# Attention and two feed-forward layers on one core: the first loads, the window bias and the mask of the opening rearranged

## The chip, the cores and the metric

The kernel runs on one core of a Trainium2 chip. The metric is device time in microseconds. Before the change three runs gave a median of 640.09 us (639.93 to 641.4).

The engines are called PE (TensorE, matrix products, with PEld for its weight loads), DVE (VectorE), ACT (ScalarE), POOL (GpSimd) and SP (SyncE, which here only issues DMAs). Each has its own instruction queue and works through it in the order in which the program was written. SPq and ACTq are the queues from which DMAs are issued.

## The reference

Attention over 2 batches, 8 heads, 768 positions and 64 values a head, with a window and a few global keys, then two feed-forward layers over 1536 tokens:

```python
scores = q @ k.T / 8
rel = pos[:, None] - pos[None, :]
is_global = pos[None, :] < n_global          # 8
is_local = (rel >= 0) & (rel < n_local)      # 96
dist = where(is_global & ~is_local, n_local, abs(rel))
slopes = 2.0 ** (-8 * (arange(8) + 1) / 8)
scores = where(is_global | is_local, scores - slopes[h] * dist, -1e9)
x = softmax(scores) @ v                      # then (1536, 512)
h = x @ w_in;   y = max(0.01 * h, h) @ w_out                 # layer 1
h = y @ w2_in;  out = (P(h) / (Q(h) + 1e-6)) @ w2_out        # layer 2, P and Q with coefficients a, b
```

n_global and n_local are 64-bit integers that the kernel reads from memory. The weights come as 64-bit floats and are decoded to 32-bit on the chip.

## The kernel before

A head pair (two heads of one batch) is one of 8 steps of the attention. In a pair, each of 6 blocks of 128 query rows and each of the 2 heads is a unit, 12 units a pair and 96 in all. A unit compares its 128 queries with 128 window columns (block 0) or 256 (32 global keys and the previous block's last 96 in the first half, its own block in the second).

Values are kept in two 32-bit halves, "high" and "low" (qh, ql, kh, kl), so a score is three products: qh·kh, qh·kl, ql·kh (L379). To get there, q and k rows are loaded (L286), transposed on PE with the identity matrix (L308), copied to the high half on ACT (L318, L347), and subtracted for the low half on DVE (L320, L349). `prep_slots` (L336 on POOL, L333 on ACT) then copies the previous block's and the global keys' columns into the free places between the blocks.

A unit's steps are: scores on PE, `least` on DVE (L390, adds the head's bias and takes the least), `exp` on ACT (L404), transposes on PE (L415), `evacuate` on ACT or DVE (L421, L423), `values` on PE (L434 to L437), and `finish` on DVE after every three blocks (L443 to L446). The main loop (L570 to L592) runs over slots n; in slot n it emits scores of n, least of n, exp of n - 1, transposes of n - 3, values of n - 5, and then `fillers(n)`: the loads and preparation of the next pair, one of the six late biases, the decoding of weights. So the order of work on each engine is written out by hand. The two units of a slot share a score bank with the units two slots later, and a group of scores waits for the least before it.

The opening, in program order:

- ACT issues two DMAs that spread the integers over 128 partitions (L92, L93); SP issues eight loads of 96 KB, the first pair's q and k in halves of three blocks, in the order q, q, k, k, q, q, k, k (L458 to L460).
- PE runs 18 products of a constant tile that nothing reads (`keep_busy`, BUSY), later 3, 2 and 2 more at other places.
- the first halves are transposed; then `window_bias` (L213) makes the distances for all 384 columns, reads the integers (L99 to L103), makes a mask of -8e9 beside them and clips the distances. A head's bias is dist times slope plus mask, one DVE instruction over 384 columns (L241). Head 0 comes before the first least, head 1 between the first and the second, heads 2 to 7 in slots 1, 2, 4, 5, 8 and 9.
- after the first halves SP goes on to the second pair's k (2 loads of 192 KB), the first pair's v (6 loads), the second pair's q (2 loads of 192 KB; its buffer is single, so it waits until the first pair's q has been transposed).
- in slot 0 the second halves are transposed; in slot 1 they are copied and subtracted; units 4 and 5 (third block) still work on the first half.
- the second pair's k and q are transposed in slots 4 and 5 (PREP0).

After the attention come the two layers, 96 units of 512 tokens by 128 columns, two product groups a unit (L621, L742, L744).

```python
            for n in range(8):
                next(halves[n // 2 % 2])
            keep_busy(BUSY[0])
            q0, k0, q1, k1 = P_[0].prep_q(0), P_[0].prep_k(0), P_[0].prep_q(1), P_[0].prep_k(1)
```

Of the kernel before, what the change touches and what calls it, by code (L numbers as in the profile page):

```python
# [8 lines left out]
F32 = mybir.dt.float32  # L9
F32R = mybir.dt.float32r  # L10
# [9 lines left out]
MAX_LOCAL = P - GW + 1  # L20
QK_BOUND = 7000.0
EPS_Q = 1.0 + 1e-6


@with_exitstack
def attention_moe_moe2(
# [67 lines left out]
    intf = cpool.tile([P, 4], F32, name="intf")  # L94
    nums = cpool.tile([P, 2], F32, name="nums")
    n_loc = nums[:, 0:1]
    n_glo = nums[:, 1:2]

    def read_ints():  # L99
        nc.vector.tensor_copy(intf, ints)  # L100
        lo, hi = (intf.rearrange("p (j w) -> p j w", w=2)[:, :, w] for w in range(2))
        nc.vector.scalar_tensor_tensor(hi, lo, 0.0, hi, ALU.is_lt, ALU.add)
        nc.vector.scalar_tensor_tensor(nums, hi, 4294967296.0, lo, ALU.mult, ALU.add)  # L103

    coef = cpool.tile([P, 8], F32, name="coef")

# [73 lines left out]
    def decode_all(rpool, dpool, wt, w_in, w_out, f):  # L180
        for m, src in enumerate(weight_srcs(w_in, w_out, f)):
# [6 lines left out]
            split_hi(wt[:, 2 * m, :], t.t)  # L188
            split_lo(wt[:, 2 * m + 1, :], t.t, wt[:, 2 * m, :])

    zeros = cpool.tile([P, 1], F32, name="zeros")
    nc.vector.memset(zeros, 0.0)
    eight = cpool.tile([P, 1], I32, name="eight")
# [18 lines left out]

    def window_bias(bpool, rpool):  # L213


        misc = rpool.tile([P, 2 * DM], I32, tag="raw", name="misc")
        misc2 = rpool.tile([P, 2 * DM], F32, tag="raw", name="misc2")
        rel_i = misc[:, 0:BW]
        dist = misc.bitcast(F32)[:, BW : 2 * BW]
        mask = misc2[:, 0:BW]  # L220
        nc.gpsimd.iota(rel_i[:, 0:W2], [[-1, W2]], base=P, channel_multiplier=1)
        nc.gpsimd.iota(rel_i[:, W2:BW], [[-1, P]], base=0, channel_multiplier=1)
# [8 lines left out]
        read_ints()  # L231

        nc.vector.tensor_scalar(mask, dist, n_loc, -8e9, ALU.is_ge, ALU.mult)
        mask_g = misc2[:, 0 : 2 * W2].rearrange("p (a c) -> p a c", a=2)[:, :, 0:GW]
        col_g = col.unsqueeze(1).to_broadcast([P, 2, GW])
        nc.vector.scalar_tensor_tensor(mask_g, col_g, n_glo, mask_g, ALU.is_ge, ALU.mult)
        nc.vector.tensor_scalar(dist, dist, n_loc, None, ALU.min)
        bias = bpool.tile([P, H, BW], F32, name="bias")

        def head(h):  # L240
            nc.vector.scalar_tensor_tensor(  # L241
                bias[:, h, :], dist, -8.0 * 2.0 ** (-8.0 * (h + 1) / H), mask, ALU.mult, ALU.add
            )

        return bias, head

    def attention(wpool, w1, ffn):
        with ExitStack() as actx:
# [26 lines left out]
            class Pair:  # L275
# [62 lines left out]
                def prep_q(self, s):  # L338
                    if s == 0:
                        self.qt = apool.tile([P, S], F32, tag="qt", name="qt", bufs=1)  # L340
                        self.qh, self.ql = (apool.tile([P, S], F32R, tag=n, name=n) for n in ("qh", "ql"))
                    cs = slice(s * HALF, (s + 1) * HALF)
                    t = self.transposed(self.qr, s).rearrange("p i c -> p (i c)")
                    yield
                    hi, lo, w = self.qh[:, cs], self.ql[:, cs], self.qt[:, cs]
                    if self.n == 0:
                        nc.scalar.activation(hi, t, AF.Copy)  # L347
                        yield
                        nc.vector.tensor_tensor(lo, t, hi.bitcast(F32), ALU.subtract)  # L349
                        return  # L350
# [3 lines left out]
                    nc.gpsimd.tensor_tensor(lo, w, hi.bitcast(F32), ALU.subtract)  # L354

                def x_out(self, s):
                    yield from x_steps(ffn.bank(), self.xp, self.b, self.hp, s)
# [97 lines left out]
                p.st, p.o = {}, {}  # L455
            U = [Unit(n) for n in range(PU * len(pairs))]

            halves = [P_[0].load("qr", q, HB), P_[0].load("kr", k, HB)]  # L458
            for n in range(8):
                next(halves[n // 2 % 2])  # L460
# [10 lines left out]
            q0, k0, q1, k1 = P_[0].prep_q(0), P_[0].prep_k(0), P_[0].prep_q(1), P_[0].prep_k(1)  # L471
            next(q0)
            next(k0)
            next(q0)
            next(k0)
            keep_busy(BUSY[1])
            bias, bias_head = window_bias(bpool, rpool)
            next(q0, None)
            next(k0)
            bias_head(0)  # L480
            next(k0, None)
            P_[1].load_k()
            P_[0].load_v()
            P_[1].load_q()
# [33 lines left out]
            def fillers(n):  # L518
# [21 lines left out]
                if p == 0 and s in BIAS:  # L540
                    bias_head(2 + BIAS.index(s))
# [28 lines left out]
            while n < len(U) or running or n <= len(U) + LV + 1:  # L570

                for m in GROUPS.get(n, ()):
                    for step, _ in enumerate(zip(unit(m).scores(), unit(m + 1).scores())):
# [501 lines left out]
```

## Time and profile before

| | before |
|---|---|
| median of 3 runs | 640.09 us |
| profiled execution, its own time | 639.84 us |
| its span | 638.0 us |
| PE busy | 626.7 us (98%) |
| DVE busy | 472.8 us (74%) |
| ACT busy | 438.1 us (69%) |
| POOL busy | 208.3 us (33%) |

The span is the part of the execution that the profile covers; 1.84 us lie around it. In a timeline row the columns are start, duration, engine, line, operation, output<-inputs, shapes and count, and in brackets the idle time of the engine just before, with what ended it. Times are in us from the start of the span. In a table of stretches the columns are the stretch, its length, each engine's busy time with its count of instructions, the granted PE clock, the mean share of the 16 DMA engines and GB/s (a share can pass 1 where packets overlap).

### The profile page before, as it was taken

Reading aid. Unit: us, or ns where it says so; the run is one execution under the profiler, and the core shown is the slowest. Engines: PE = TensorE matmul, PEld = TensorE weight load, DVE = VectorE, ACT = ScalarE, POOL = GpSimd, SP = SyncE. Lnnn points to the kernel's source line nnn. Section 1 sums busy time; section 2 is a strip of 40 time slices with the busy share of each in tenths; the row PEclk is TensorE's granted clock in tenths of the full one; section 3 lists DMA queues with packets and bytes.
Section 4 is the critical chain, followed back from the end, with each engine's and each line's share of the span. In section 5 each row is a group of like instructions: output and inputs, shape, how many; then the busy total and the mean of one; then the engine's idle time right before and its main releaser. Section 6 shows DMA issues by size and latency. Waiting matters only on the chain.

```text
span 638.0 us, 9653 instructions
## 1 busy us (share of the span) xinstructions
PE 626.7 (98%) x3289; PEld 527.5 (83%) x3289; DVE 472.8 (74%) x934; ACT 438.1 (69%) x829; POOL 208.3 (33%) x221
## 2 busy tenths in 40 slices
PE   7999999999999999999999999999999999999996
PEld 6999998888888888888888888888888888888884
DVE  6888897887886555555444479897777777897784
ACT  5888987877866545455333477876677888876672
POOL 3978874344543434332000012222222222112220
PEclk9999999999999999999999999999999999999999
DMA  9876751755167776765222300000023331100001
GB/s 192 190 174 154 184 137 67 271 180 207 58 205 249 217 229 200 235 210 181 92 96 95 100 33 34 1 1 1 0 97 102 98 95 48 67 25 1 2 1 72
DMA packets 81179, 73.35 MB, mean 115 GB/s; under 512 B 51232, under 2 KB 67616, under 8 KB 81120
## 3 DMA queue, kind: packets, MB, share of 16 engines
q1 hardware_dynamic: 80320, 71.19, 37.6%
q0 software_dynamic: 224, 0.92, 0.4%
q8 instruction: 28, 0.46, 0.3%
q10 hardware_dynamic: 576, 0.53, 0.2%
q14 instruction: 31, 0.25, 0.1%
HBM read 60.69 MB, written 11.93 MB: 114 GB/s over the span
## 4 chain that ended last, share of the span: by engine, by line
PE 94%; DVE 3%; SPq 1%; DMA 1%; issue 0%; ACT 0%; DVEq 0%; ACTq 0%
PE h L621 41%; PE y L744 21%; PE y L742 20%; PE pt L415 3%; PE sc L379 3%; PE o L437 2%; PE o L436 2%; PE h L308 1%; SPq L286 1%; DVE sn L390 1%; PE h L204 1%; DMA qr<-in_q_dram 1%; DVE xl L210 0%; DVE pts L423 0%; PE o L434 0%
## 5 line engine op out<-in xcount | busy, mean ns | idle before, releaser
L621 PE MATMUL h<-xh,w 128*128 128x512 f32 x768 | 252.8, 390 | 0.0
L621 PEld LDWEIGHTS h<-xh,w 128*128 128x128 f32 x768 | 144.2, 188 | 29.7
L621 PE MATMUL h<-xl,w 128*128 128x512 f32 x384 | 149.4, 389 | 0.0
L675 POOL TENSOR_TENSOR gl<-u,gh 128x512 fp32r<-128x512 f32 x44 | 57.0, 1296 | 264.6 <-PE y L744 125.6
L742 PE MATMUL y<-gh,w 128*128 128x512 f32 x384 | 126.0, 389 | 0.0
L744 PE MATMUL y<-w,gh 128*128 128x512 f32 x384 | 125.5, 389 | 0.0
L160 POOL TENSOR_TENSOR dec<-dec,wraw 128x512 int32<-128x512 int32 x48 | 63.8, 1339 | 82.8 <-DVE wraw L147 79.1
L621 PEld LDWEIGHTS h<-xl,w 128*128 128x128 f32 x384 | 72.1, 188 | 14.8
L742 PEld LDWEIGHTS y<-gh,w 128*128 128x128 f32 x384 | 72.0, 188 | 14.9
L744 PEld LDWEIGHTS y<-w,gh 128*128 128x128 f32 x384 | 72.1, 188 | 14.8
L744 PE MATMUL y<-w,gl 128*128 128x512 f32 x192 | 75.1, 391 | 0.0
L742 PE MATMUL y<-gl,w 128*128 128x512 f32 x192 | 74.7, 389 | 0.0
L646 DVE TENSOR_TENSOR gl<-h,gh 128x512 fp32r<-128x512 f32 x48 | 33.0, 688 | 52.5 <-ACT gh L645 52.5
L645 ACT ACTIVATE gh<-h 128x512 fp32r<-128x512 f32 x48 | 28.6, 597 | 59.8 <-PE y L742 56.5
L697 ACT ACTIVATE h<-h 128x512 f32<-128x512 f32 x48 | 28.7, 597 | 52.6 <-PE h L621 52.5
L641 DVE SCALAR_TENSOR_TENSOR h<-h,g 128x512 f32<-128x512 f32 x48 | 33.3, 694 | 27.2 <-ACT g L640 27.0
L685 DVE SCALAR_TENSOR_TENSOR w<-w,epsq,h 128x512 f32<-128x512 f32 (+1 forms) x49 | 36.4, 743 | 20.9 <-ACT h L709 20.3
L640 ACT ACTIVATE g<-h 128x512 f32<-128x512 f32 x48 | 28.8, 600 | 31.1 <-PE h L621 30.9
L404 ACT ACTIVATE pr<-sn,st 128x256 f32<-128x256 f32 (+1 forms) x96 | 47.5, 496 | 1.3 <-DVE st L390 1.1
L699 DVE SCALAR_TENSOR_TENSOR w<-h,coef,w 128x512 f32<-128x512 f32 x48 | 35.9, 748 | 15.9 <-ACT w L698 15.6
L744 PEld LDWEIGHTS y<-w,gl 128*128 128x128 f32 x192 | 36.0, 188 | 8.7 <-POOL gl L675 1.1
L742 PEld LDWEIGHTS y<-gl,w 128*128 128x128 f32 x192 | 36.1, 188 | 7.5
(115 smaller groups left out, 1123.9 us busy)
## 6 DMA issues: line engine op xcount, KB each, us to landing
wraw<-in_moe_w_in_dram SPq DMA_DIRECT2D x24, 512.0 KB, 4.7
wraw<-in_moe_w_out_dram SPq DMA_DIRECT2D x24, 512.0 KB, 4.6
scratch<-dec SPq DMA_DIRECT2D x32, 256.0 KB, 5.3
wf<-scratch SPq DMA_DIRECT2D x16, 512.0 KB, 3.4
w<-in_moe_w_in_dram SPq DMA_DIRECT2D x8, 512.0 KB, 4.2
w<-in_moe_w_out_dram SPq DMA_DIRECT2D x8, 512.0 KB, 5.0
vc<-in_v_dram SPq DMA_DIRECT2D x16, 192.0 KB, 3.2
qkraw<-in_q_dram SPq DMA_DIRECT2D x6, 512.0 KB, 3.5
```

What stands on the lines that cost most here:

```text
L160: nc.gpsimd.tensor_tensor(ti, ti, self.c, ALU.add)
L404: nc.scalar.activation(self.pr[:, :w], self.sn[:, :w], AF.Exp, bias=self.least_at, scale=-1.0,)
L621: nc.tensor.matmul(h, wt[:, m, c * P : (c + 1) * P], xs[:, c, cs], start=c == 0 and n == 0, stop=c == NK - 1 and n == 2,)
L640: nc.scalar.activation(g, h, AF.Copy)
L641: nc.vector.scalar_tensor_tensor(h, h, 0.01, g, ALU.mult, ALU.max)
L646: nc.vector.tensor_tensor(gl, h, gh.bitcast(F32), ALU.subtract)
L675: (nc.gpsimd if on_pool else nc.vector).tensor_tensor(gl, g, gh.bitcast(F32), ALU.subtract)
L685: nc.vector.scalar_tensor_tensor(ow[:, cs], ow[:, cs], epsq, oh2[:, cs], ALU.add, ALU.mult)
L697: nc.scalar.activation(h2, h, AF.Square)
L699: nc.vector.scalar_tensor_tensor(w0, h2, coef[:, 7:8], w0, ALU.mult, ALU.add)
L742: nc.tensor.matmul(ys[d], wt[:, m, ds_], gs, start=st, stop=sp)
L744: nc.tensor.matmul(ys[d], gs[:, ds_], wt[:, m, :], start=st, stop=sp)
```

## The change

- The integers come to one partition only (two loads of one row), are put together there, and a product of a row of ones with them on PE spreads them over 128 partitions (`spread`, copied to `nums` by DVE).
- The first pair's q and k come in parts of two and four blocks instead of three and three, in the order q, k, k, q; of the first k part one load is issued from ACT.
- The mask is added to the clipped distance (2.56e11 where a key is excluded), so a head's bias is one product with the slope. Distances and mask get tiles of their own. They are made in two parts: the 128 columns that block 0 needs before unit 0, the other 256 after unit 1's least. Head 1's second part is made on ACT in slot 1.
- Heads 2 to 7 move to slots 7, 9, 14, 16, 26 and 28.
- Warm-up products: 12 and 3, the later ones are gone.
- Both first exps come in slot 1. The second halves are copied in slot 1, subtracted in slot 2 and their slots filled in slot 3, where before copy and subtraction were both in slot 1.

```diff
-    BUSY = (18, 3, 2, 2)
-    BIAS = (1, 2, 4, 5, 8, 9)
+    BIAS = (7, 9, 14, 16, 26, 28)
+    BUSY = (12, 3)
-    ints = cpool.tile([P, 4], I32, name="ints")
-    nc.scalar.dma_start(ints[:, 0:2], n_local.bitcast(I32).partition_broadcast(P))
-    nc.scalar.dma_start(ints[:, 2:4], n_global.bitcast(I32).partition_broadcast(P))
+    ints = cpool.tile([1, 4], I32, name="ints")
...
+    def load_ints(j, src):
+        nc.scalar.dma_start(ints[:, 2 * j : 2 * j + 2], src.bitcast(I32).partition_broadcast(1))
...
+        def far(first):
+            cs = part(first)
+            nc.vector.tensor_scalar(mask[:, cs], dist[:, cs], n_loc, FAR, ALU.is_ge, ALU.mult)
+            gs = slice(cs.start, cs.start + GW)
+            nc.vector.scalar_tensor_tensor(mask[:, gs], col, n_glo, mask[:, gs], ALU.is_ge, ALU.mult)
+        def near(first):
+            cs = part(first)
+            nc.vector.scalar_tensor_tensor(dist[:, cs], dist[:, cs], n_loc, mask[:, cs], ALU.min, ALU.add)
+        def head(h, cs=slice(0, BW), on_act=False):
+            b, slope = bias[:, h, cs], -8.0 * 2.0 ** (-8.0 * (h + 1) / H)
+            if on_act:
+                nc.scalar.activation(b, dist[:, cs], AF.Copy, scale=slope)
+            else:
+                nc.vector.tensor_scalar(b, dist[:, cs], slope, None, ALU.mult)
...
+                def load_first(self, s):
...
+                    b = slice(*((0, 2), (2, NB))[s])
+                    for name, src in (("q", q), ("k", k)) if s == 0 else (("k", k), ("q", q)):
+                        for j, queue in enumerate((nc.sync, nc.scalar if s == 0 and name == "k" else nc.sync)):
+                            r = src[self.b, 2 * self.hp + j].rearrange("(i p) d -> p i d", p=P)
+                            queue.dma_start(self.first[name][:, b, j], r[:, b])
...
+            load_ints(0, n_local)
+            load_ints(1, n_global)
+            P_[0].load_first(0)
+            P_[0].load_first(1)
...
             keep_busy(BUSY[0])
+            bias, bias_part, bias_far, bias_near, bias_head = window_bias(bpool, rpool)
+            next(q0)
+            read_ints()
+            spread = ps.tile([P, W2], F32, tag="pt", name="spread")[:, 0:2]
+            nc.tensor.matmul(spread, ones, num1, start=True, stop=True)
+            next(k0)
+            keep_busy(BUSY[1])
             next(q0)
             next(k0)
+            nc.vector.tensor_copy(nums, spread)
+            bias_far(True)
             next(q0, None)
             next(k0)
             next(k0, None)
+            bias_near(True)
+            for h in range(2):
+                bias_head(h, bias_part(True))
...
                 if n == 1:
-                    next(k1)
-                    next(q1, None)
+                    bias_head(1, bias_part(False), on_act=True)
...
-                        if n == 0 and step == 0:
-                            keep_busy(BUSY[2], P // 2)
-                    if n == 2:
-                        keep_busy(BUSY[3])
...
-                    if m == 0:
-                        bias_head(1)
-                if unit(n - 1):
-                    unit(n - 1).exp()
+                    if m == 1:
+                        bias_far(False)
+                        bias_near(False)
+                        bias_head(0, bias_part(False))
+                for m in (0, 1) if n == 1 else (n - 1,):
+                    if n != 2 and unit(m):
+                        unit(m).exp()
```

## Rows read from the trace of the kernel before

**Rows 1.** The page: busy time, share and instructions of PE; chain by engine.

```profile
PE 626.7 (98%) x3289; PEld 527.5 (83%) x3289; DVE 472.8 (74%) x934; ACT 438.1 (69%) x829; POOL 208.3 (33%) x221
PE 94%; DVE 3%; SPq 1%; DMA 1%; issue 0%; ACT 0%; DVEq 0%; ACTq 0%
```

**Rows 2.** Waits of PE, whole span: total us, times, longest us.

```profile
PE pt L415 <- DVE pts L423: 1.1, 3, 0.6
PE h L308 <- DMA qr<-in_q_dram: 1.0, 2, 0.6
```

**Rows 3.** Table of stretches, from the second pair's q on.

```profile
14.46:20.00 5.54, 5.44 (x54) 4.99 (x55) 4.49 (x17) 3.98 (x10) 4.02 (x8) 1.00 0.73 135
20.00:36.00 16.00, 16.00 (x162) 15.06 (x160) 14.32 (x59) 13.54 (x37) 13.60 (x21) 1.00 0.88 211
```

**Rows 4.** Chain of waits, in order of time: start, us, what.

```profile
10.19 3.61 DMA qr<-in_q_dram
```

**Rows 5.** Table of stretches, opening: read the last two columns.

```profile
2.00:4.00 2.00, 2.00 (x12) 2.00 (x10) 1.37 (x4) 1.01 (x1) 0.31 (x3) 1.00 0.36 70
4.00:5.25 1.25, 0.99 (x7) 0.79 (x6) 0.28 (x2) 0.00 (x0) 0.00 (x0) 1.00 1.04 228
11.00:13.80 2.80, 1.94 (x14) 1.50 (x14) 2.67 (x11) 2.29 (x8) 0.00 (x0) 1.00 1.22 240
```

**Rows 6.** DMA issues of the first 2.7 us: KB each, us to landing.

```profile
qr<-in_q_dram SPq DMA_DIRECT2D x1, 96.0 KB, 4.0
kr<-in_k_dram SPq DMA_DIRECT2D x2, 96.0 KB, 3.7
```

**Rows 7.** Timeline of the opening.

```profile
0.73 1.00 SPq L286 DMA_DIRECT2D qr<-in_q_dram  x2
4.94 0.17 DVE L100 CAST intf<-ints 128x4 f32<-128x4 int32 x1 [1.25 <-DMA ints<-in_n_global_dram]
5.37 0.52 PE L308 MATMUL h<-ident,qr 128*128 128x128 f32 x3 [0.37 <-DMA qr<-in_q_dram]
8.38 0.29 DVE L390 CUSTOM_DVE_ANT_0 sn<-sc,bias 128x128 f32<-128x128 f32 x1 [0.15 <-DVE bias L241]
13.94 0.52 PE L308 MATMUL h<-ident,qr 128*128 128x128 f32 x3 [0.60 <-DMA qr<-in_q_dram]
```

**Rows 8.** Groups, first 20 us (last: page): count, busy us, mean ns, idle.

```profile
L390 DVE CUSTOM_DVE_ANT_0 sn<-sc,bias 128x256 f32<-128x256 f32 x10 | 3.8, 418 | 1.6 <-PE sc L379 1.5
L320 DVE TENSOR_TENSOR kl<-h,kh 128x384 fp32r<-128x384 f32 x3 | 1.7, 552 | 0.0
L227 DVE TENSOR_SCALAR misc<-misc 128x384 f32<-128x384 f32 x1 | 0.4, 362 | 0.0
L318 ACT ACTIVATE kh<-h 128x384 fp32r<-128x384 f32 x4 | 1.9, 483 | 0.2 <-PE h L308 0.2
L333 ACT ACTIVATE kl<-kl 128x288 fp32r<-128x288 f32 x1 | 0.4, 444 | 0.6 <-DVE kl L320 0.6
L645 ACT ACTIVATE gh<-h 128x512 fp32r<-128x512 f32 x48 | 28.6, 597 | 59.8 <-PE y L742 56.5
```

**Rows 9.** Timeline of PE in narrow windows: the constant products.

```profile
1.27 0.58 PE L468 MATMUL idle<-warm 128*128 128x256 f32 x1 [1.27 <-DVE warm L463]
1.27 1.44 PE L468 MATMUL idle<-warm 128*128 128x256 f32 x5 [1.27 <-DVE warm L463]
4.60 0.40 PE L468 MATMUL idle<-warm 128*128 128x256 f32 x2
4.72 0.28 PE L468 MATMUL idle<-warm 128*128 128x256 f32 x1
```

**Rows 10.** Timeline of DVE and POOL around late biases.

```profile
17.78 0.86 DVE L241 SCALAR_TENSOR_TENSOR bias<-misc,misc 128x384 f32<-128x384 f32 x1
17.40 0.83 POOL L353 TENSOR_TENSOR qh<-qt,zeros 128x384 fp32r<-128x384 f32 x1
37.88 0.42 DVE L390 CUSTOM_DVE_ANT_0 sn<-sc,bias 128x256 f32<-128x256 f32 x1 [0.99 <-PE sc L379]
```

More of the change, by code (lines that the diff above doesn't have):

```diff
@@ L22 @@
 EPS_Q = 1.0 + 1e-6
+FAR = 2.56e11
 @with_exitstack
@@ L88, in attention_moe_moe2 @@
     xpool = ctx.enter_context(tc.tile_pool(name="xpool", bufs=1))
-    ints = cpool.tile([P, 4], I32, name="ints")
-    nc.scalar.dma_start(ints[:, 0:2], n_local.bitcast(I32).partition_broadcast(P))
-    nc.scalar.dma_start(ints[:, 2:4], n_global.bitcast(I32).partition_broadcast(P))
-    intf = cpool.tile([P, 4], F32, name="intf")
+    ints = cpool.tile([1, 4], I32, name="ints")
+    intf = cpool.tile([1, 4], F32, name="intf")
+    num1 = cpool.tile([1, 2], F32, name="num1")
+    ones = cpool.tile([1, P], F32, name="ones")
     nums = cpool.tile([P, 2], F32, name="nums")
@@ L189, in decode_all @@
             split_lo(wt[:, 2 * m + 1, :], t.t, wt[:, 2 * m, :])
+    nc.vector.memset(ones, 1.0)
     zeros = cpool.tile([P, 1], F32, name="zeros")
@@ L230, in window_bias, with part @@
         nc.vector.tensor_copy(col, col_i)
[L231 to L237, printed above, removed]
-        bias = bpool.tile([P, H, BW], F32, name="bias")
[L240 to L245, printed above, removed]
+        bias = bpool.tile([P, H, BW], F32, name="bias")
+        def part(first):
+            return slice(W2, BW) if first else slice(0, W2)
+        def far(first):
[12 more added lines that the diff above has]
+                nc.vector.tensor_scalar(b, dist[:, cs], slope, None, ALU.mult)
+        return bias, part, far, near, head
     def attention(wpool, w1, ffn):
@@ L354, in prep_q @@
                     nc.gpsimd.tensor_tensor(lo, w, hi.bitcast(F32), ALU.subtract)
+                def load_first(self, s):
+                    if s == 0:
+                        self.first = {
+                            n: apool.tile([P, NB, 2, D], F32, tag=f"{n}r", name=f"{n}r", bufs=2 if n == "k" else 1)
+                            for n in "qk"
+                        }
+                    b = slice(*((0, 2), (2, NB))[s])
[3 more added lines that the diff above has]
+                            queue.dma_start(self.first[name][:, b, j], r[:, b])
@@ new lines, in transposed_first, with prep_first_k, places @@
+                def transposed_first(self, name, s):
+                    b0, b1 = ((0, 2), (2, NB))[s]
+                    t = ffn.bank()[:, : (b1 - b0) * P].rearrange("p (b c) -> p b c", c=P)
+                    for b in range(b0, b1):
+                        nc.tensor.transpose(t[:, b - b0], self.first[name][:, b].rearrange("p r d -> p (r d)"), ident)
+                    return t
+                def prep_first_k(self, s):
+                    if s == 0:
+                        self.kh = apool.tile([P, (2 * NB - 1) * P], F32R, tag="kh", name="kh")
+                        self.kl = apool.tile([P, (2 * NB - 1) * P], F32R, tag="kl", name="kl")
+                    b0, b1 = ((0, 2), (2, NB))[s]
+                    def places(t):
+                        if s == 0:
+                            return t[:, 0 : 2 * W2].rearrange("p (b c) -> p b c", c=W2)[:, :, 0:P]
+                        c0 = 2 * W2 - P
+                        return t[:, c0 : c0 + 4 * W2].rearrange("p (b c) -> p b c", c=W2)[:, :, P:W2]
+                    t = self.transposed_first("k", s)
+                    yield
+                    nc.scalar.activation(places(self.kh), t, AF.Copy)
+                    yield
+                    nc.vector.tensor_tensor(places(self.kl), t, places(self.kh.bitcast(F32)), ALU.subtract)
+                    yield
+                    self.prep_slots((b0, min(b1, NB - 1)))
@@ new lines, in prep_first_q @@
+                def prep_first_q(self, s):
+                    if s == 0:
+                        self.qh, self.ql = (apool.tile([P, S], F32R, tag=n, name=n) for n in ("qh", "ql"))
+                    cs = slice(0, W2) if s == 0 else slice(W2, S)
+                    hi, lo = self.qh[:, cs], self.ql[:, cs]
+                    t = self.transposed_first("q", s).rearrange("p b c -> p (b c)")
+                    yield
+                    nc.scalar.activation(hi, t, AF.Copy)
+                    yield
+                    nc.vector.tensor_tensor(lo, t, hi.bitcast(F32), ALU.subtract)
@@ L456, in attention @@
             U = [Unit(n) for n in range(PU * len(pairs))]
-            halves = [P_[0].load("qr", q, HB), P_[0].load("kr", k, HB)]
-            for n in range(8):
-                next(halves[n // 2 % 2])
+            load_ints(0, n_local)
+            load_ints(1, n_global)
+            P_[0].load_first(0)
+            P_[0].load_first(1)
+            first = P_[0]
+            q0, k0, q1, k1 = first.prep_first_q(0), first.prep_first_k(0), first.prep_first_q(1), first.prep_first_k(1)
             warm = bpool.tile([P, W2], F32R, name="warm")
@@ L539, in fillers @@
                             new.append(P_[p - 1].x_out(half))
-                if p == 0 and s in BIAS:
-                    bias_head(2 + BIAS.index(s))
+                if n in BIAS:
+                    bias_head(2 + BIAS.index(n))
                 if n in DECS and early:
@@ L572, in attention @@
                 for m in GROUPS.get(n, ()):
-                    for step, _ in enumerate(zip(unit(m).scores(), unit(m + 1).scores())):
-                        if n == 0 and step == 0:
-                            keep_busy(BUSY[2], P // 2)
-                    if n == 2:
-                        keep_busy(BUSY[3])
+                    for _ in zip(unit(m).scores(), unit(m + 1).scores()):
+                        pass
                 for m in LEASTS.get(n, ()):
                     unit(m).least()
-                    if m == 0:
-                        bias_head(1)
-                if unit(n - 1):
-                    unit(n - 1).exp()
+                    if m == 1:
[5 more added lines that the diff above has]
+                        unit(m).exp()
                 if unit(n - 3):
```

20 lines of the change are left out of this document (4 added, 16 removed).

## The prediction

> **What bounds the kernel now.** I read the page first: PE is busy 626.7 of 638.0 us and holds 94% of the chain that ended last [rows 1]. The reader is to see that only time in which PE is idle, or does work that the result does not need, can be won. The waits of PE over the whole span come next: apart from the first 15 us there is almost nothing, 1.1 us for evacuated probabilities in three places and 1.0 us for loads of q in two [rows 2]. The table of stretches then says where the opening ends: from 14.46 us on PE is busy 5.44 of 5.54 us and then 16.00 of 16.00 [rows 3]. PE works through its queue in order, so whatever the change does, it is worth the amount by which PE reaches the point of 14.46 us earlier, plus the small stalls behind it.
>
> What sets that point is told by the chain of waits: a load of the second pair's q, issued at 10.19 us, took 3.61 us and landed at 13.80 [rows 4]. PE had stood idle for 0.60 us when it transposed that q at 13.94 [rows 7], so it was ready at 13.34. The DVE work ahead of unit 0's least, at 8.38 us, is what the change shortens; the row shows that least waiting for a bias [rows 7]. But that chain had 0.60 us to spare against the load.
>
> Why did the load take 3.61 us, when it is 192 KB? The DMA share is 1.04 from 4.00 us and still 1.22 up to 13.80 [rows 5]: the engines have no gap. First pair's q and k 768 KB, second pair's k 384, first pair's v 704 and second pair's q 384 make 2240 KB, or 2.29 MB. At 228 to 240 GB/s that is 9.6 to 10.1 us; with 140 kB moved in 2.00 to 4.00 (70 GB/s for 2 us) the remaining 2.15 MB end between 13.0 and 13.4, plus the time from the last byte to the landing. The row says 13.80, so this load is set by bytes, not by when it is issued.
>
> **The loads (two queues, parts of two and four blocks).** Bytes and order to the second pair's q are the same; SP has 17 issues ahead of its end instead of 18, one less at (10.19 - 0.73) / 17 = 0.56 us [rows 4, 7]. If the load followed its issue, it would land 0.56 us earlier; if it follows the bytes from 4.00 us on, not at all. Between them lies the slow start: 70 GB/s in 2.00 to 4.00 against 228 after [rows 5]; each us of full rate won there moves all that follows by about 0.7. The two loads of integers with 128 rows each, which run in that start, also go. I take half of the issue, -0.3 us: landing at 13.5. ACT's own issue of a k part comes before its first copy, which waits for PE anyway.
>
> On this the Trainium skill ("DMA: Bandwidth & Descriptors", section "Issuing engines are not separate DMA queues") says that loads issued from several engines run on the same 16 DMA engines and interleave, so that a second issuer saves only the time to issue. By that rule alone the second queue would win nothing at 13.80, and the sum would be 640.1 us; the share of 1.22 agrees, the slow start is where the row leaves room.
>
> The first q and k themselves do come earlier. Before, q is 197 kB: 140 kB by 4.00 and the rest at 228 GB/s make 4.25, landed at 1.24 + 4.0 = 5.24 us [rows 5, 6], so about 1 us passes from byte to landing. With k, 393 kB: 5.1, landed at 2.3 + 3.7 less the spread of the two, about 5.9. Now q is 131 kB (3.9, lands about 4.85) and with k 262 kB (4.55, lands about 5.4). That is 0.4 to 0.5 us; bounds 0 (same landing) and 0.9 (the byte-to-landing time shrinks too).
>
> **The integers.** One row each instead of 128. DVE idled 1.25 us until 4.94 for them [rows 7]. The product needs them before PE can go on: behind it in PE's queue stand the k transposes, three constant products and the scores, and DVE's copy of the result holds q's and k's subtractions behind it. If they land by 4.5 us, their three small DVE steps end before q is transposed (5.2), at no cost. If they land at 4.9 as before, the product runs at about 5.5 and PE loses 0.3. I take 0 on the sum, since the load of q covers it. The row of ones is one more tiny DVE fill.
>
> **When PE is ready for the second pair's q.** From k at 5.4, with ACT copies of 0.26, 0.37, 0.48 and 0.60 us for 128 to 512 columns, and DVE steps of 0.29, 0.42, 0.55 and 0.69 (the rows for 256, 384 and 512, with the same step down and up) [rows 8]: k transposed 5.8, kh 6.2; DVE copies the numbers, masks 128 columns, subtracts q and k until 6.75, then the clipped distance and two products on 128 columns (0.29 + 2 x 0.2, taken between nothing and the 0.36 of 384 columns): 7.35. Leasts 0 and 1 to 7.95, against 8.38 for the first before. Then the other 256 columns: mask, clip and head 0, four DVE steps, about 1.0: 8.95. Least 2 to 9.4. Least 3 needs head 1's second part, which stands on ACT behind two exps (about 0.4 each, as copies of 256 columns) and two copies of 512 columns (0.60 each): about 10.05, so least 3 ends at 10.45. Now the cost of the parts of two and four: units 4 and 5 need the second part, whose subtractions come in slot 2 (two of 512 columns, 1.2 us: 11.65) and whose k slots come in slot 3 on ACT (0.44 for 288 columns and a small one, about 0.6, from the first subtraction at 11.05: 11.65). The last four products of units 4 and 5 end at 12.15, and with the transposes of two units, of k and one set of values, about 1.0 us, PE is ready at 13.1. Before it was 13.34: nearly all that is won at unit 0 is given back at units 4 and 5. Bounds: 12.7 with the first loads 0.4 earlier still, 13.6 with none earlier.
>
> 13.1 lies before 13.5, so the landing decides.
>
> **Late heads, folded mask, fewer constant products.** Four biases leave the DVE queue before slot 6 (0.55 each, as L320 of the same width), where the landing hides the gain. The two that stood in slots 8 and 9 go to 7 and 9 and get cheaper. Four go to slots 14 to 28, where DVE is busy 14.32 of 16.00 us [rows 3]. A product over 384 columns took 0.36 [rows 8]. Beside POOL the old form took 0.86: it started at 17.78 in slot 8 and POOL's instruction ran until 18.23 [rows 10], 0.45 us of waiting. So one costs 0.36 to 0.36 + 0.83, nearer 0.6 or 0.7; the 1.68 us in which DVE idles in 20 to 36 [rows 3] and 0.99 us at 36.9 to 37.9 [rows 10] cover it. Price if not: a part of 4 x 0.65 = 2.6 us. Constant products are on no path from 4.25 on; fewer of them cost nothing unless the clock minds (below). The swapped iotas and the separate tiles are hidden behind the loads. All this: 0, between -0.4 (the 0.10 us missing from 5.54 and some of the 1.1 us of PE's waits for DVE go [rows 2, 3]) and +0.6.
>
> **Sum.** 639.84 (profiled execution: 638.0 span and 1.84 around it) - 0.3 = 639.5. The median lies 0.25 above the profiled execution, so 639.8 us. What a measurement can tell here is about 0.3%, 1.9 us: faster would be below 638.2, slower above 642.0.
>
> **Rivals.**
> 1. The start of the loads is what is late, and its whole gain passes on: landing at 13.2, the small stalls gone: -1.0, 639.1 us. For it: only 70 GB/s until 4.00. Against: no DMA gap after that. Chance 0.20.
> 2. Nothing moves: the transfers start as before or the integers hold PE for 0.3 to 0.5 us, and the landing stays at 13.80: 640.1. Chance 0.15.
> 3. The clock of PE. The constant products start 0.215 us apart ((1.44 - 0.58) / 4), which is the level of 1.2 GHz for 256 columns, and 0.12 apart at 4.60 to 4.72, the level of 2.4 [rows 9]; PE had worked without a gap since 1.27. With 12 products PE falls idle at about 4.0, before that rise. If it stays at 1.2 GHz, PE's share of the ready chain doubles: about 1.2 us up to the first scores and 1.94 in 11.00 to 13.80 [rows 5], so ready at 13.1 + 3.1 = 16.2, 2.7 us past the landing: 642.5. It decides once the rise comes later than about 8 us; before that the 0.4 us of reserve hide most of it. Against it: PE still has two thirds of its old work in this stretch. Chance 0.08.
> 4. The heads in slots 14 to 28 meet POOL and lag PE: two of them past the cover, about 2 x 0.65, so 641.1. For it: POOL is busy 13.60 of 16.00 [rows 3]. Chance 0.10. The Trainium skill ("SBUF — State Buffer", section "Who interferes with whom") has DVE and POOL share one pair of ports that is held for a whole instruction; by that rule the new form would wait as long as the old, up to 1.2 us each, and the row at 17.78 agrees with the wait.
>
> The forecast itself has 0.47: 639.8, its own range 639.2 to 640.4. The range takes in rivals 1, 2 and 4 and leaves out 3: 638.7 to 641.3. Faster: only if rival 1 goes past its bound, 0.08. Slower: rival 3 and the end of 4, 0.10. Same: 0.82.
>
> **What would show it.** In the profile after, first q transposed near 5.0 and unit 0's least near 7.5 (loads and bias right); units 4 and 5 near 12 us, no earlier than before (the slots given back); the second pair's q transposed near 13.6 after an idle wait for its load (the landing decides). Wrong if PE reaches it without a wait, if that load lands before 13.0, if scores of 256 columns start 0.21 us apart after 8 us, or if PE waits for evacuated probabilities between 20 and 40 us by more than 0.5 us.

## Result: slower by 0.8%

The changed kernel took 645.86 us (median of 6 runs, 645.16 to 646.93), the kernel before 640.01: a ratio of 1.0079 with an interval of 1.0059 to 1.0098. The forecast was 639.8 and "same"; the time lies outside its range. Of the profiled executions the span went from 638.0 to 644.1 us.

The page of the changed kernel, the lines that answer to [rows 1], and its waits of PE, which answer to [rows 2]:

```profile
PE 633.5 (98%) x3281; PEld 533.0 (83%) x3281; DVE 473.3 (73%) x940; ACT 439.6 (68%) x830; POOL 208.0 (32%) x221
PE 93%; DVE 4%; DMA 1%; issue 1%; ACT 0%; SPq 0%; DVEq 0%; ACTq 0%
```

```profile
PE pt L470 <- DVE pts L478: 1.1, 3, 0.6
PE h L318 <- DMA qr<-in_q_dram: 1.0, 2, 0.7
PE sc L434 <- DVE st L445: 0.8, 3, 0.4
```

PE is busy 6.8 us longer with fewer instructions. Such a thing is not a wait: look for work that ran slower. The table of stretches has those of [rows 5] and [rows 3] first, then those in which the clock changes:

```profile
2.00:4.00 2.00, 2.00 (x11) 1.96 (x10) 1.62 (x7) 1.28 (x1) 0.31 (x2) 1.00 0.70 157
4.00:5.25 1.25, 1.25 (x7) 0.85 (x5) 0.11 (x1) 0.38 (x1) 0.00 (x0) 1.00 0.99 225
11.00:13.80 2.80, 2.33 (x14) 1.57 (x14) 2.13 (x8) 2.24 (x8) 0.00 (x0) 1.00 1.39 208
14.46:20.00 5.54, 5.54 (x32) 4.64 (x33) 2.09 (x8) 2.01 (x6) 3.27 (x6) 0.50 1.07 152
20.00:36.00 16.00, 15.30 (x128) 14.35 (x129) 11.89 (x43) 11.38 (x28) 10.74 (x16) 0.86 0.62 143
14.00:14.50 0.50, 0.05 (x1) 0.08 (x2) 0.00 (x0) 0.50 (x3) 0.00 (x0) 0.61 1.39 218
14.50:24.00 9.50, 9.50 (x51) 8.60 (x52) 4.41 (x17) 3.92 (x11) 4.72 (x8) 0.50 0.62 89
24.00:24.50 0.50, 0.50 (x5) 0.50 (x5) 0.26 (x1) 0.50 (x2) 0.00 (x0) 0.65 0.00 0
```

From about 14.1 to 24.4 us the granted clock is 0.50, so 1.2 GHz, while PE is busy all the time. Before, 14.46 to 20 us held 54 matmuls [rows 3]; now the same stretch holds 32 at an equal busy time. The other thing to see is the row of 11.00 to 13.80: the DMA engines are busier than before (1.39 against 1.22) and move less (208 against 240 GB/s). Each byte has become dearer.

The opening in the timeline, to lay beside [rows 7], and the load in the chain of waits, beside [rows 4]:

```profile
4.09 0.66 PE L377 MATMUL h<-ident,qr 128*128 128x128 f32 x2
7.53 0.29 DVE L445 CUSTOM_DVE_ANT_0 sn<-sc,bias 128x128 f32<-128x128 f32 x1
9.71 0.41 PE L434 MATMUL sc<-kl,qh 64*128 64x256 f32 x2
9.93 0.41 PE L434 MATMUL sc<-kh,ql 64*128 64x256 f32 x2
10.95 0.63 PE L434 MATMUL sc<-kh,qh 64*128 64x256 f32 x2 [0.21 <-DVE st L445]
11.81 0.38 PE L434 MATMUL sc<-kl,qh 64*128 64x256 f32 x2 [0.22 <-DVE kl L396]
12.40 0.38 PE L434 MATMUL sc<-kh,ql 64*128 64x256 f32 x2 [0.21 <-DVE ql L409]
12.82 0.42 DVE L445 CUSTOM_DVE_ANT_0 sn<-sc,bias 128x256 f32<-128x256 f32 x1 [0.47 <-PE sc L434]
14.45 0.87 PE L318 MATMUL h<-ident,qr 128*128 128x128 f32 x3 [0.69 <-DMA qr<-in_q_dram]
```

```profile
9.86 4.46 DMA qr<-in_q_dram
```

The first q comes in two loads, one a head. [rows 6] has the second of them alone, 4.0 us; the first took 3.1. Here are both of the changed kernel, with the median of their times to landing:

```profile
qr<-in_q_dram SPq DMA_DIRECT2D x2, 64.0 KB, 2.3
```

They land in 2.3 us instead of 3.5 in the median. The first q is transposed 1.28 us earlier than before (5.37 to 4.09). It does not wait for its load any more: PE has no gap between its first constant product and 10.7 us, and with 18 constant products instead of 12 the same transposes start at 5.18 and 4.98 (e1 and e2 below). Unit 0's least starts at 7.53 (8.38 before), and the second pair's q, issued 0.33 us earlier, takes 4.46 us instead of 3.61 and is transposed 0.51 us later than before.

The start of each pair's first scores says where the 6.1 us are. Second pair: 25.28 us against 20.55, so the opening costs 4.73. The second pair lasts 13.19 us against 11.85 (+1.34), the third 12.92 against 12.27 (+0.65). The later pairs agree to 0.1 us. What lies behind takes 0.6 us less, which is no more than executions differ: from the first product of the layers to the end of the span the 18 profiled executions of this document take 532.2 to 533.3 us.

### The profile page after: what moved, and what is told of

It is laid out like the page before. It is cut to its first block, busy times and chain, and to the rows that moved or that the text cites. A ratio compares the mean times of both kernels' runs of the same rounds, so it can differ in the third digit from the quotient of the medians.

```text
span 644.1 us, 9644 instructions
## 1 busy us (share of the span) xinstructions
PE 633.5 (98%) x3281; PEld 533.0 (83%) x3281; DVE 473.3 (73%) x940; ACT 439.6 (68%) x830; POOL 208.0 (32%) x221
## 4 chain that ended last, share of the span: by engine, by line
PE 93%; DVE 4%; DMA 1%; issue 1%; ACT 0%; SPq 0%; DVEq 0%; ACTq 0%
PE h L683 40%; PE y L806 20%; PE y L804 20%; PE sc L434 3%; PE pt L470 3%; PE o L492 2%; PE o L491 1%; DMA qr<-in_q_dram 1%; PE h L318 1%; DVE sn L445 1%; PE idle L525 1%; PE h L208 1%; DVE pts L478 0%; PE h L377 0%; DVE xl L214 0%
## 5 line engine op out<-in xcount | busy, mean ns | idle before, releaser
L804 PEld LDWEIGHTS y<-gh,w 128*128 128x128 f32 x384 | 72.1, 188 | 15.1
L806 PEld LDWEIGHTS y<-w,gh 128*128 128x128 f32 x384 | 72.1, 188 | 14.8
L761 DVE SCALAR_TENSOR_TENSOR w<-h,coef,w 128x512 f32<-128x512 f32 x48 | 35.9, 748 | 15.9 <-ACT w L760 15.6
L445 DVE CUSTOM_DVE_ANT_0 sn<-sc,bias 128x256 f32<-128x256 f32 (+1 forms) x96 | 33.9, 396 | 12.5 <-PE sc L434 12.4
```

Source lines behind the costliest of these rows:

```text
L445: nc.vector.tensor_tensor_reduce(self.sn[:, :w], self.sc[:, :w], bias[:, 2 * self.pair.hp + self.j, b0 : b0 + w], -0.125, 3.0e38, ALU.add, ...
L761: nc.vector.scalar_tensor_tensor(w0, h2, coef[:, 7:8], w0, ALU.mult, ALU.add)
L804: nc.tensor.matmul(ys[d], wt[:, m, ds_], gs, start=st, stop=sp)
L806: nc.tensor.matmul(ys[d], gs[:, ds_], wt[:, m, :], start=st, stop=sp)
```

## The experiments

Three things are in question: the rate of the loads, PE's clock, and the late heads. All ratios are to the kernel before, run beside.

**Products.** e1 and e2 give the changed kernel constant products back, e3 takes them from the kernel before.

```diff
-    BUSY = (12, 3)          # e1: changed kernel
+    BUSY = (18, 3)
-    BUSY = (12, 3)          # e2: changed kernel, with the old calls of BUSY[2] and BUSY[3]
+    BUSY = (18, 3, 2, 2)
-    BUSY = (18, 3, 2, 2)    # e3: kernel before
+    BUSY = (12, 3, 0, 0)
```

> The changed kernel with 18 constant products at the start instead of 12. Theory (the clock of PE: it rises late and falls near 14 us because the constant products are gone): with the clock at its upper level from about 4.4 us and held, 639.5 us (639 to 640.5); if it rises early but falls again near 14 us, 644 to 646. Rival 1 (the second pair's q lands at 14.3 instead of 13.8 and later loads follow): stays at 644 or more with no stretch at 1.2 GHz. Rival 2 (the moved heads and the parts of two and four cost it): stays at 644 or more.

> The changed kernel with all constant products of the old one (18, 3, 2, 2 at the old places). Theory clock: 639.5 us (638.8 to 640.6), granted clock 1.00 in 14 to 24 us. Rivals (late loads; moved heads and parts): 644 or more although the clock holds. Against the kernel with 18 at the start alone it tells whether the four small ones hold the clock.

> The kernel before with 12 and 3 constant products and none at the two later places, nothing else changed. Theory clock: 644 to 647 us, with a stretch at 1.2 GHz near 14 to 24 us. Rivals (the rest of the change costs it): 640, as before.

e1: 643.49 us, 1.0064 (1.0040 to 1.0087). e2: 644.14, 1.0066 (1.0043 to 1.0089). e3: 642.01, 1.0030 (1.0020 to 1.0040). So fewer products alone cost the kernel before 2.3 us, less than was expected. Giving them back wins 1.7 to 2.4 of the 5.9 by the medians, though single runs of e1 (up to 646.63) and e2 (up to 646.00) are as slow as the changed kernel's. In e3's profiled execution PE stands at 1.2 GHz from 8 to 21.5 us with nothing else changed. It is the slowest of e3's nine (643.72; the others 641.24 to 642.41), so it does not show what the others lose:

```profile
8.00:14.00 6.00, 5.73 (x29) 4.48 (x28) 5.28 (x20) 4.20 (x13) 1.38 (x3) 0.50 1.19 243
14.46:20.00 5.54, 5.54 (x33) 4.64 (x32) 1.83 (x7) 2.51 (x7) 3.31 (x6) 0.50 0.68 131
```

**Idle time of PE.** e4 puts 8 constant products ahead of the second pair's q, e7 fills all gaps of the opening.

```diff
+                if n == 5:                       # e4 and e7, in fillers
+                    keep_busy(8)
...
+                        if n == 4 and step < 2:  # e7, among the scores
+                            keep_busy((5, 3)[step])
+                    if n == 2:
+                        keep_busy(10)
```

> The changed kernel with 8 more constant products just ahead of the transposes of the second pair's q, where PE sat idle 0.7 us. The late rise (near 11 us) stays. Theory clock, if the fall near 14.1 us is what costs: 640.5 to 641.5, no fall. If the late rise costs by itself: 643 or more. Rivals: 645 as the changed kernel.

> The changed kernel with 18 constant products first and more of them wherever PE waits between 9 and 14.5 us: 10 after the scores of units 2 and 3, 5 and 3 inside those of units 4 and 5, 8 ahead of the second pair's q. Theory clock: granted clock 1.00 throughout and 639.5 to 641, what is left over being the later landing. Theory placement as the main cost: 643 or more even with the clock held.

e4: 643.64 us, 1.0060 (1.0043 to 1.0076); the clock fell at 12.4, before the products, and was back at 15.9, so the run does not test the products at that place. e7 (with 18 products first): 643.33, 1.0050 (1.0038 to 1.0062); its profile has no fall, but the products themselves held PE until the second pair's q at 16.23, and a wait of 1.0 us for the third pair's q came behind. The fall is gone with the idle time; what fills it costs as much.

**Addresses.** The change adds a tile of 8 bytes (num1, which takes 32) and a row of ones (512 bytes) ahead of all other tiles. In the built programs first and second pair's q and k lay on multiples of 512 bytes before (first q at 142848) and start 32 bytes past one after (146464). e5 puts num1 and intf into one tile, so that the shift is 512 (146432); e6 gives the kernel before an unused tile of 32 bytes (142880).

```diff
-    intf = cpool.tile([1, 4], F32, name="intf")     # e5: changed kernel
-    num1 = cpool.tile([1, 2], F32, name="num1")
+    both = cpool.tile([1, 6], F32, name="both")
+    intf, num1 = both[:, 0:4], both[:, 4:6]
...
+    cpool.tile([P, 8], F32, name="pad")             # e6: kernel before
```

> The changed kernel with the two small integer tiles in one, so that every later tile is moved by 512 bytes against the kernel before instead of 544. Nothing else. Theory placement (the transfers are slowed because the tiles that they write now start 32 bytes off a multiple of 64): 235 to 260 GB/s in 8 to 14 us instead of about 210, the second pair's q lands near 13.0 to 13.3, and with the shorter wait the clock falls later or not at all: 640 to 643. Theory clock alone (few constant products and idle of PE in the reordered preparation): rates may rise, but the fall near 14 us stays: 644 to 646.

> The kernel before with a tile of 32 bytes that nothing uses, which moves every later tile by 32 bytes. Theory placement: about 210 GB/s in 8 to 14 us instead of 237, the second pair's q lands at 14.8 instead of 13.8, 641 us if the clock holds, 644 if the longer wait makes it fall. Theory clock alone: 640, as before.

e5: 642.39 us (10 runs), 1.0046 (1.0029 to 1.0064), 3.5 us less than the changed kernel. e6: 644.25 us (10 runs), 1.0058 (1.0039 to 1.0077), with no instruction changed. The stretch of the third line of [rows 5] in e5 and in e6, and e6's load in its chain:

```profile
11.00:13.80 2.80, 2.76 (x11) 1.95 (x12) 2.07 (x8) 1.91 (x7) 0.00 (x0) 1.00 1.19 262
```

```profile
11.00:13.80 2.80, 2.07 (x16) 1.50 (x14) 2.67 (x12) 2.30 (x8) 0.01 (x1) 1.00 1.35 202
14.46:20.00 5.54, 4.60 (x25) 3.96 (x27) 1.67 (x6) 1.79 (x5) 2.21 (x5) 0.56 1.23 186
```

```profile
10.86 4.41 DMA qr<-in_q_dram
```

The 32 bytes take the rate from 240 to 202 GB/s and bring a loss like the changed kernel's about: load 4.41 us long, PE idle 1.74 us for it, clock 0.50 behind it. Two of e6's ten runs, 640.78 and 641.36, have a mean granted clock of 0.997; the other eight, 643.01 to 645.34, have 0.989 to 0.993. So the late load by itself costs some 1.2 to 1.8 us, and the fall of the clock the rest. That the destination's address is what slows the loads is shown both ways, and every trace agrees: in the stretch of the third line of [rows 5] the eight executions with tiles 32 bytes past the multiple move 202 to 220 GB/s at a share of 1.32 to 1.39, nine on it 240 to 262 at 1.10 to 1.23 (the tenth, e12, moves 192 at a share of 0.88). The Trainium skill ("DMA: Bandwidth & Descriptors", section "How a descriptor splits into AXI transactions") has the first transaction of a piece of a transfer that does not start on a multiple of 256 bytes begin at the multiple below, so that bytes are fetched that nobody uses; it says so of reading, and here only the side that is written moved. The runs agree in direction: a larger share for fewer bytes.

**Both, with the old order.** e8 is e5 with e2's products.

> The changed kernel with the shift of 512 bytes and all the constant products of the old one (18, 3, 2, 2). If both the placement and the clock count: 639 to 640.3, the clock held and the second pair's q at 13.0 to 13.3. If it stays at 643 or more, the idle of PE in the reordered preparation alone makes the clock fall.

643.27 us, 1.0054 (1.0030 to 1.0078): a miss, near the expectation's second branch. At full clock PE waits 1.19 us for the leasts of units 2 and 3, and the clock falls at 13.7.

**Late heads.** e9 is e5 with the heads early; e13 is the changed kernel with them early; e10 is e9 with e2's products and the second parts' subtractions one slot earlier (in its expectation "the last" is e9).

```diff
-    BIAS = (7, 9, 14, 16, 26, 28)
+    BIAS = (4, 5, 6, 7, 8, 9)               # e9, e10, e13
...
                 if n == 1:
+                    next(k1)                 # e10
+                    next(q1, None)
                     bias_head(1, bias_part(False), on_act=True)
```

> The changed kernel with the shift of 512 bytes, and heads 2 to 7 in slots 4 to 9 instead of 7 to 28. Theory (late heads cost): in the shift_512 run the second pair took 12.69 us and the third 12.91, before 11.85 and 12.27; with the heads out of them the two come back to about 11.9 and 12.3, 1.4 us less, and the time is 642.4 - 1.4 = 641.0 us. Rival (late heads cost nothing, the two pairs are long for another reason, such as where the opening leaves the pipeline): pairs 2 and 3 stay at 12.7 and 12.9 and the time at 642.4. Second rival: the heads in slots 4 to 9 delay the leasts of the opening by as much as they free later, pair 1 grows by 0.5 or more.

> The changed kernel with heads 2 to 7 in slots 4 to 9 and nothing else (tiles still moved by 544 bytes). If the late heads cost what the third pair shows (12.92 against 12.27 us), 645.9 - 0.65 = 645.2 us. If they also cost what stands between the shift_512 run and the one with early heads (642.4 - 640.5), 644.0. If nothing, 645.9. In each case the clock falls near 14 us and the second pair starts later than 24 us; rival: without the late heads it does not fall, and the time is near 641.

> As the last, with the constant products of the kernel before (18, 3, 2, 2) and the subtractions of the second parts of k and q back one slot earlier (slot 1). Theory (PE's clock and the late heads are the whole loss once the addresses are put right): units 4 and 5 come early, PE has no long idle time ahead of the second pair's q, the clock stays at 2.4 GHz, second pair starts near 20.5 us as before, time 639.5 to 640.0. Rival (the new order of the opening itself leaves PE idle for over 1 us, whatever the products): the clock falls again within 18 us, second pair at 22 or later, time 641.5 to 643.

e9: 640.47 us (12 runs), 1.0013 (1.0000 to 1.0026). e13: 643.57, 1.0047 (1.0028 to 1.0065). By the medians the heads' place is worth 1.9 us at the right addresses and 2.3 at the shifted ones. Part of that is the clock: e9's profile reaches the second pair 1.20 us before e5's, and e13's 1.73 us before the changed kernel's. The third pair shows the heads cleanly: 12.92 us in the changed kernel and 12.91 in e5, 12.26 and 12.27 in e13 and e9, as before. The second pair is 12.06 in e13, but 12.80 in e9, where 0.77 us of wait for the third pair's q took the heads' place:

```profile
24.05 0.52 PE L318 MATMUL h<-ident,qr 128*128 128x128 f32 x3 [0.77 <-DMA qr<-in_q_dram]
```

A head beside POOL in the changed kernel, to lay beside the first two of [rows 10], and its place in the chain of waits:

```profile
32.35 1.16 DVE L253 TENSOR_SCALAR bias<-dist 128x384 f32<-128x384 f32 x1
31.95 1.33 POOL L359 TENSOR_TENSOR ql<-qt,qh 128x384 fp32r<-128x384 f32 x1
29.91 0.35 DVE L253 TENSOR_SCALAR bias<-dist 128x384 f32<-128x384 f32 x1
```

```profile
32.43 1.08 DVE bias L253
```

1.16 us, and 0.35 where POOL is idle; the row stands in the chain, and no idle time of DVE covers it. The Trainium skill ("SBUF — State Buffer", section "Who interferes with whom") has the one that comes second wait for the whole instruction of the other, and the row agrees: the head ends at 33.51, 0.23 us behind POOL's. Two of the six heads, one in the second pair and one in the third, meet POOL so.

e10 is a miss: 642.06 us, 1.0027 (1.0014 to 1.0041). The subtractions of 512 columns (0.68 us each) now stand on DVE ahead of the leasts of units 2 and 3, and PE waits for those; the clock falls at 13.9 and the second pair starts at 22.29, as the rival had it:

```profile
12.76 0.64 PE L434 MATMUL sc<-kh,qh 64*128 64x256 f32 x2 [2.17 <-DVE st L445]
```

**The start of the loads.** e11 is the kernel before with its first two k loads issued by ACT; e12 is e5 with the integers loaded by 128 rows each, of which row 0 is used.

```diff
+                            queue = nc.scalar if self.n == 0 and name == "kr" and i == 0 else nc.sync   # e11
...
-    ints = cpool.tile([1, 4], I32, name="ints")       # e12, with partition_broadcast(P)
+    ints = cpool.tile([P, 4], I32, name="ints")
```

> The kernel before, with the first pair's first two k loads issued from ACT's queue and nothing else. Theory A (the second queue alone makes the faster start): 139 GB/s or more in 2 to 3 us against 67, first q transposed at 4.1 to 4.6 instead of 5.37, second pair's q transposed near 13.4 instead of 13.94, time 639.2. Theory B (the integer loads with 128 rows hold the start back): 67 to 80 GB/s in 2 to 4 us as before, q at 5.3, time 639.7 as before.

> The changed kernel with the shift of 512 bytes, its integers loaded by 128 rows each as before (row 0 alone is used). Theory A (second queue makes the start): 140 to 190 GB/s in 2 to 4 us, q transposed at 4.1. Theory B (the 128-row loads hold it back): 67 to 80 GB/s in 2 to 4 us, q transposed at 4.8 to 5.4; the integers' product also comes later, at 4.9 or after.

e11: 640.23 us, 1.0002 (0.9992 to 1.0011). The stretch of the first line of [rows 5] in e11, then in e12:

```profile
2.00:4.00 2.00, 2.00 (x12) 2.00 (x10) 1.37 (x4) 1.28 (x1) 0.32 (x3) 1.00 0.38 74
```

```profile
2.00:4.00 2.00, 2.00 (x11) 1.97 (x10) 1.37 (x4) 1.28 (x1) 0.32 (x2) 1.00 0.33 62
```

The second queue by itself wins no time (in its one trace the second pair's q lands at 13.44, 0.36 us earlier, and PE comes to it at 14.18); the two loads of 128 short rows hold the first us down. Without them the same stretch carries 157 to 169 GB/s. (e12 is one run of 646.19 us, with PE at 1.2 GHz from 1.33 to about 23.2 us.)

**Program or execution.** e14, e15 and e16 are e5, e9 and the changed kernel once more.

> The shift_512 kernel once more, for a second profile: its first had PE at 1.2 GHz from 1.33 to 16.9 us. Theory (the rise follows from the program): again no rise before 16 us, second pair from 21.8. Rival (the moment of the rise differs between executions of one program): a rise at another time, and the start of the second pair moves by about half of the difference after the second pair's q.

> The shift_512 kernel with early heads once more: its first profile had the rise at 4.5 us, although its PE instructions up to 10 us are those of the shift_512 kernel. Theory (program): rise at 4.5 again, second pair from 20.6. Rival (execution): no rise until 14 us or later, second pair from 21 to 22.

> The changed kernel once more: its first profile had a rise near 11 us, the fall at 14.1 and the next rise at 24.3. Theory: the same three times within 0.5 us, since its six times lie between 645.2 and 646.9. Rival: one of them differs by over 1 us.

640.82, 643.64 and 645.57 us. The moment of the first rise differs between executions of one program: in e5 a single transpose still takes 0.47 us at 12.86 and the rise comes at 16.9; in e14 it comes near 10.5. In e9 it was at 4.3 and in e15 at 6.2, in the changed kernel at 10.7 and in e16 at 6.0:

```profile
12.86 0.47 PE L470 MATMUL pt<-ident,pr 128*128 128x128 f32 x1
16.91 0.28 PE L470 MATMUL pt<-ident,pr 128*128 128x128 f32 x1
```

```profile
12.35 0.38 PE L434 MATMUL sc<-kh,ql 64*128 64x256 f32 x2 [0.21 <-DVE ql L409]
13.55 0.49 PE L318 MATMUL h<-ident,qr 128*128 128x128 f32 x3
```

The Trainium skill ("TensorE: Matmul & The Clock Gate", section "What's actually happening") calls the moment of the rise variable from run to run, and these traces agree; where it puts a size to this, half a microsecond either way, they lie up to 6 us apart (e5 and e14). In the second execution of the changed kernel (e16) PE was at full clock from 6.0 us, waited 1.49 us, and the clock fell sooner:

```profile
10.52 0.64 PE L434 MATMUL sc<-kh,qh 64*128 64x256 f32 x2 [1.49 <-DVE st L445]
```

```profile
12.50:13.00 0.50, 0.50 (x6) 0.50 (x5) 0.50 (x3) 0.35 (x2) 0.00 (x0) 0.83 1.40 218
13.90:23.00 9.10, 9.09 (x49) 8.20 (x50) 4.41 (x17) 3.96 (x10) 4.71 (x8) 0.50 0.64 97
```

What the clock costs is read from one table (us; fall and rise from the granted clock of half-us stretches, in e5 from the durations of transposes):

| execution | second pair's q transposed | clock low | second pair's first scores | between |
|---|---|---|---|---|
| before | 13.94 | not | 20.55 | 6.61 |
| changed | 14.45 | 14.1 to 24.4 | 25.28 | 10.83 |
| changed again (e16) | 13.91 | 12.8 to 23.1 | 24.38 | 10.47 |
| e6 | 15.40 | 15.1 to 25.4 | 26.26 | 10.86 |
| e13 | 13.99 | 11.0 to 21.3 | 23.55 | 9.56 |
| e2 | 14.43 | 14.8 to 21.6 | 23.80 | 9.37 |
| e5 | 14.52 | until 16.9 | 21.82 | 7.30 |
| e14 | 13.55 | until about 10.5 | 19.88 | 6.33 |
| e9 | 13.83 | 11.2 to 14.6 | 20.62 | 6.79 |
| e9 again (e15) | 13.62 | 13.1 to 23.3 | 24.34 | 10.72 |
| e7 | 16.23 | not | 22.54 | 6.31 |

The work between the two points takes 6.3 to 6.6 us at full clock, and a little less than half of the low time that falls in it comes on top; e1, e3, e4, e8, e10 and e11 fit as well. e14 is close to the forecast's opening: q at 13.55 (forecast 13.6), the second pair 0.67 us earlier than before. Of the four profiled executions with few products and the addresses right (e5, e14, e9, e15) one opened so; of the two of the changed kernel none did, and its six timed runs, with a mean granted clock of 0.989 to 0.993, look like those two.

**What PE did before the clock fell.** The sum of its idle time does not tell. In the kernel before PE idles 1.57 us between 9 and 14 us, and the clock holds; the pieces are 0.60 us for the second pair's q [rows 7] and these two:

```profile
9.65 0.38 PE L379 MATMUL sc<-kh,qh 64*128 64x256 f32 x1 [0.39 <-DVE st L390]
11.39 0.73 PE L379 MATMUL sc<-kh,qh 64*128 64x256 f32 x2 [0.58 <-DVE st L390]
```

Waits in one piece tell more. In the new order, where the clock was up by about 7 us, PE ran ahead and then waited 1.19 to 2.17 us at once for the leasts of units 2 and 3 (e1, e2, e4, e8, e9, e10, e13, e15, e16). In all nine the clock fell 0.6 to 3.8 us after the wait. In e7 constant products leave 0.29 us of it, and the clock holds. In e6 PE waits 1.74 us for the late load, and the clock falls in that wait. Where the rise came only near 10.5 us (the changed kernel's first profile and e14) the waits there are 0.2 to 0.3 us each; the changed kernel then waits 0.69 us for the second pair's q and falls, e14 does not wait for it and holds. So by these traces the changed kernel falls in two ways, and the late load has a part in one of them only. Short waits leave it open: e11, with 0.38 and 0.58 us, falls at 13.2.

## Why the prediction was wrong

**What held.** Unit 0's least was forecast near 7.5 and came at 7.53. That is in part luck: the first q was transposed 1.28 us earlier, where 0.4 to 0.5 was forecast and 0.9 was the bound, but q, the integers' product and the constant products stood before k in PE's queue, at 1.2 GHz and without a gap, so that k's transposes ended at 5.88, near the 5.8 of the sum. Units 4 and 5 were forecast near 12 and no earlier than before; unit 4's least is at 12.82, against 12.28. The integers cost nothing: their product waits for PE, not for them. PE is the bound, and only its idle or slowed time counts: so it was.

**The landing, -0.3 us: not seen.** "Bytes and order to the second pair's q are the same" counted the issues and the bytes and not where the bytes go. The shift of 32 bytes takes the rate to 202 to 220 GB/s. The load landed at 14.32 instead of 13.5, and at 13.77 in e16, against 13.80 before. With the addresses put right the load lands earlier than forecast, at 13.15 in e14. The 13.55 of q there agrees with the forecast's 13.6 by luck: the forecast had PE ready at 13.1 and waiting, and in e14 PE comes to a load that is there, which the forecast had named as a sign of being wrong. The faster start that the term credited in part to the second queue belongs to the integers' narrow loads (e11, e12).

**The clock, cost 0 and rival 3 at 642.5 with 0.08: the step that failed.** The price was for a first rise that does not come until 8 us, and its bill ended at the second pair's q. That rise came at 10.7 us in the changed kernel's first profile (the scores at 9.71 and 9.93 start 0.21 us apart, a named sign of being wrong) and at 6.0 in e16, and both are slow. The runs showed something else in its place: PE, which idles 1.3 and 2.2 us in these two between 9 and 14.5 us, in waits for the leasts and for the load, falls to 1.2 GHz and stays there for 10 us in a stretch where it is the bound. That is 10.83 us instead of 6.61: +4.2 of the 6.1 us. "Fewer of them cost nothing" is 2.3 us in e3. The forecast's own sum had gaps of PE at units 2 to 5 and did not ask what they do to the clock. It also had PE ready for the second pair's q at 13.1, at most 13.6; PE was ready at 13.76, and at 13.67 in e16, so the landing at 13.5 would not have decided.

**The late heads, cost 0: wrong by 0.65 us in the third pair alone, by 1.9 to 2.3 us in the medians with what moves in the opening.** Rival 4 had the mechanism and the number of heads, two; it priced such a head at 0.65 us, and it took 1.16 against 0.35. The step that failed is the cover: DVE's idle time of 1.68 us lies at other moments than the heads, and around them the chain runs through DVE.

**What the sum looks like now.** In the changed kernel: opening 4.73, of which 0.51 at the second pair's q and 4.22 behind it, second pair 1.34, third 0.65, behind them -0.6. The causes do not add: addresses (3.5 between changed kernel and e5, 3.1 between e13 and e9), products (1.7 to 2.4) and heads (1.9 to 2.3) make 6.7 to 8.2 of 5.9 us. That they act on the same fall of the clock is the likely reason; no run takes their shares apart. Address and heads together explain 5.4 (e9, at 640.47, is on a level with the kernel before). No kernel here beats the kernel before by what can be measured.

**What stays open.** What decides the moment of the first rise; why some short waits are followed by a fall and others are not, and why the clock is back soon in e9 (low from 11.2 to 14.6) and not in e15 (13.1 to 23.3); why a wait of 0.2 to 1.0 us for the third pair's q appears in most of the other executions, e3 and e11 among them, and not before.

## What to carry to other kernels

A small tile that is added ahead of others moves all of them: look at the address of every tile that a DMA fills, before and after (here the multiple of 512 and 32 bytes past it were tried; no run tells whether a smaller multiple is enough). Where PE is the bound, price each us of its idle time at the clock too: the stretch behind the gap, not the gap, is what the clock doubles. Idle time of an engine covers an added instruction only if it lies at that moment; look for the instruction's neighbours in the chain of waits.

## What was not expected of the hardware

- Rows of 256 bytes that land 32 bytes past a multiple of 512 are moved at 202 to 220 GB/s with the DMA engines busier (a share of 1.32 to 1.39), on the multiple at 240 to 262 (1.10 to 1.23).
- Two loads of 128 rows of 8 bytes hold other loads to 62 to 78 GB/s for 2 us; with one row each it is 157 to 169.
- The record of the granted clock reads 1.00 from the start of the trace until its first event: in e12 it is 1.00 throughout, while scores of 256 columns start 0.21 us apart until 21 us. The spacing of equal matmuls is the surer row there.
